# Raw weight loads issued by ScalarE behind earlier scalings, with a third raw place and five float32 places

## The chip, the cores and the metric

One core of a Trainium2 chip runs the kernel. The metric is the device time in microseconds, from launch to end. Engines are named as in the profile: PE (TensorE), DVE (VectorE), ACT (ScalarE), POOL (GpSimd), SP (SyncE).

## The reference

An attention with a threshold, and then two layers one after the other, each of two products with a function between them. The four weight matrices (`w_in` and `w_out` of each layer) come as float64, everything else as float32.

```python
def _attn_ref(q, k, v, tau):                 # 4 batches, 8 heads, 576 rows, 64 wide
    scores = scale * np.matmul(q, k.transpose(0, 1, 3, 2))
    thresh = np.max(scores, axis=-1, keepdims=True) - tau
    scores = np.where(scores >= thresh, scores, -1000000000.0)
    scores = scores - np.max(scores, axis=-1, keepdims=True)
    attn = np.exp(scores)
    attn = attn / (np.sum(attn, axis=-1, keepdims=True) + 1e-09)
    return np.matmul(attn, v).astype(np.float32)

def _moe_ref(x, w_in, w_out, a, b):          # 2304 tokens, 512 -> 2048 -> 512
    h = x @ w_in
    P = a[0] + a[1] * h + a[2] * h2 + a[3] * h3
    Q = 1.0 + np.abs(b[0]) * np.abs(h) + np.abs(b[1]) * h2
    return ((P / (Q + 1e-06)) @ w_out).astype(np.float32)

def _moe2_ref(x, w_in, w_out):
    h = x @ w_in
    g = np.where(pos, h, np.where(neg, 0.0, (h + beta) ** 2 / (4.0 * beta)))
    return (g @ w_out).astype(np.float32)

x = attention, heads side by side;  return _moe2_ref(_moe_ref(x))
```

## The kernel before

**Stages.** The tokens are worked on by batch (4), and each batch by three blocks of 192 tokens. For each batch the order is attention, first layer, second layer; the steps of a layer are 3 blocks x 8 chunks of the inner width. A step makes its first product (`first_product`, the matmuls of L843), the function (`rational` for the first layer, its first instruction is L724; `quadratic` for the second), and three steps later its second product (`second_product`, L857). The attention of the next batch runs beside the layers of the present one. The first batch's attention has a form of its own (`first_attention`), and beside it the weights are made.

**Weights.** Each of the two layers has 8 chunks, each chunk a half from `w_in` (x = 0) and one from `w_out` (x = 1): 32 halves, counted here from 0 to 31 in their order. Halves 0 to 15 belong to the first layer (`make_half`), 16 to 31 to the second (`stage_half`). A half is loaded raw (L241, 1024 KB, on SP), turned from float64 bits into float32 by three DVE instructions (`as_float`, L228 to L230), squared on PE (L253) for a bound on its size (L254, L187, L188), from which DVE makes a power of two (`root`, L168 to L172). ACT scales the float32 half in place (L217), and `split` makes two float16 parts of it, the high one on ACT (L208) and the low one by four subtractions on POOL (L212). The parts of the first layer stay in `wc` tiles and are also stored (L265); those of the second go into one of two `wh` tiles and are stored (L270), to be loaded when the second layer begins (L277).

**Buffers.** Raw halves lie in the tag "rw", two places; the raw `v` of the next batch (`prep_v`, L300 and L298) uses the same two. Float32 halves lie in "wt", three places (N_WT), the float16 halves of the second layer in "wh", two (N_WH). The q and k of a head pair lie raw in "rqk" and as float16 in "qk", one place each (`prep_pair`). All squares and bounds share one PSUM place, "aux".

**Order.** Instructions get a priority (`at`), and a planner that runs when the program is built lists them for each engine by readiness and priority. Buffers go round in the order of the source. Each engine and each queue then works its list in order: an instruction that waits holds up what is behind it. `tc.issue_after(ins)` puts what is issued in its block behind `ins` in the list of that engine, without a wait for its end.

Of the kernel before, what the change touches and what calls it, by code (L numbers as in the profile page):

```python
# [11 lines left out]
I32 = mybir.dt.int32  # L12
BF16 = mybir.dt.bfloat16
AF = mybir.ActivationFunctionType
# [21 lines left out]


ATTENTION = {1: (18, 50), 2: (60, 100), 3: (108, 147)}
WEIGHTS = (0, 20)
# [3 lines left out]
def tile_attention_moe_moe2(  # L43
# [20 lines left out]
    P = 128  # L64
# [140 lines left out]
    def split(hi, lo, src, scale=None, on_vector=True):  # L205
# [7 lines left out]
        elif on_vector:  # L213
            A.activation(hi, src, AF.Copy, scale=scale)
            V.scalar_tensor_tensor(lo, src, scale, hi, op0=ALU.mult, op1=ALU.subtract)
        else:
            A.activation(src, src, AF.Copy, scale=scale)  # L217
            split(hi, lo, src)

    def as_float(raw, name):  # L220

        if not wide:
            return raw
        src = raw.rearrange("p (n w) -> p n w", w=2)
        t = mp.tile([P, E], I32, name="wt" + name, tag="wt", bufs=N_WT)
        V.tensor_scalar(t, src[:, :, 1], 0x07FFFFFF, 3, op0=ALU.bitwise_and, op1=ALU.logical_shift_left)  # L228
        V.scalar_tensor_tensor(t, src[:, :, 1], -0x40000000, t, op0=ALU.bitwise_and, op1=ALU.bitwise_or)
        V.scalar_tensor_tensor(t, src[:, :, 0], 29, t, op0=ALU.logical_shift_right, op1=ALU.bitwise_or)  # L230
        return t.bitcast(F32)

    def convert(m, i, x, dst, on_vector):

        if x == 0:
            raw = rp.tile([P, KT, CF * words], raw_type, name=f"rw{m}_{i}_0", tag="rw")
            src = w_in_dram[m][:, i * CF * words : (i + 1) * CF * words].rearrange("(kt p) f -> p kt f", p=P)
        else:
            raw = rp.tile([P, NF, DM * words], raw_type, name=f"rw{m}_{i}_1", tag="rw")
            src = w_out_dram[m][i * CF : (i + 1) * CF, :].rearrange("(f p) d -> p f d", p=P)  # L240
        Q.dma_start(raw, src)  # L241
        name = f"{m}_{i}_{x}"
        src = as_float(raw.rearrange("p a b -> p (a b)"), name)
        hi, lo = dst[:, 0:E], dst[:, E : 2 * E]
# [10 lines left out]
        s = root("pw" + name, f_w[m][x][:, i : i + 1], everywhere("mw" + name, bound, 1), 2.0**64, even=m == 1 and x == 1)  # L255
        split(hi, lo, src, s, on_vector)
        if i == NCH - 1 and (m, x) != (0, 0):
# [700 lines left out]
```

## Time and profile before

| | us |
|---|---|
| median of 3 runs | 1245.84 |
| lowest, highest | 1241.46, 1250.6 |
| the profiled execution | 1242.5 |
| its span, first to last instruction | 1240.7 |
| busy PE, DVE, ACT, POOL | 1091.9, 977.1, 842.9, 543.0 |

The profile is of one execution. Busy time is a sum over the span; which engine sets the time differs from stage to stage. A row of the timeline gives start and length in us, the engine, the line of the kernel, and in brackets how long the engine was idle before it and what ended that. A half is found in the timeline by counting its line's instructions from the start.

### The profile page before, as it was taken

To read this page: it belongs to the slowest core of one execution; us is meant where nothing else is said; L and a number is where in the kernel's file an instruction comes from. 1 tells how busy PE (TensorE), PEld (TensorE's weight loads), DVE (VectorE), ACT (ScalarE), POOL (GpSimd) and SP (SyncE) were. 2 spreads that over 40 slices of the span, in tenths; PEclk is the share of its full clock that TensorE was granted. 3 is DMA by queue.
4 is the path that set the end of the run, shared out by engine and by line. 5 is a ranking of instruction groups with operands and counts; after the bars stand their busy time and mean duration, and the time that the engine had idled before them with its cause. 6 is when DMAs were issued, how large, how long until landed. Compare 5 with 4: busy or idle time off the path is not lost.

```text
span 1240.7 us, 31727 instructions
## 1 busy us (share of the span) xinstructions
PE 1091.9 (88%) x12618; PEld 984.5 (79%) x12618; DVE 977.1 (79%) x2353; ACT 842.9 (68%) x1533; POOL 543.0 (44%) x700
## 2 busy tenths in 40 slices
PE   2787788588799999999888998998899999999998
PEld 1444455488688888899788898998788989999997
DVE  7767887899997777799997776899996768896431
ACT  2477776779785677777875776887766767775332
POOL 3424545675673556421464555223563653222221
PEclk9797898799899999999999999999999999999999
DMA  7656676734447465923596539513993478007000
GB/s 209 230 169 217 218 258 205 240 116 120 108 136 234 68 125 116 249 73 92 144 238 131 110 69 245 140 49 68 243 192 69 86 167 221 14 1 259 16 14 27
DMA packets 220341, 176.40 MB, mean 142 GB/s; under 512 B 182048, under 2 KB 193312, under 8 KB 212000
## 3 DMA queue, kind: packets, MB, share of 16 engines
q1 hardware_dynamic: 220192, 174.36, 52.7%
q8 instruction: 99, 1.62, 0.5%
q14 instruction: 50, 0.41, 0.1%
HBM read 106.83 MB, written 21.50 MB: 103 GB/s over the span
## 4 chain that ended last, share of the span: by engine, by line
PE 35%; DVE 19%; DMA 9%; ACT 6%; POOL 6%; issue 6%; SPq 1%; DVEq 0%; ACTq 0%; POOLq 0%
PE ph L843 15%; PE acc L857 15%; DMA eT<-hl 7%; POOL hl L395 3%; DVE e L384 2%; PE pv L410 2%; DVE t L731 2%; DVE t L726 2%; DVE sc L422 2%; DVE t L737 1%; DMA qkT<-qk 1%; DVE t L728 1%; POOL gg L212 1%; DVE t L727 1%; ACT hl L392 1%
## 5 line engine op out<-in xcount | busy, mean ns | idle before, releaser
L857 PE MATMUL acc<-gg,wc 128*128 128x192 f16 x4608 | 427.6, 247 | 9.8 <-POOL gg L212 6.4
L843 PEld LDWEIGHTS <-wc 128*128 128x128 f16 x4608 | 389.8, 99 | 37.4 <-issue 20.8
L857 PEld LDWEIGHTS <-wc 128*128 128x128 f16 x4608 | 383.4, 98 | 13.3 <-issue 12.0
L212 POOL TENSOR_TENSOR gg<-t,gg 128x384 f16<-128x384 f32 x192 | 193.3, 1008 | 380.0 <-ACT gg L208 330.0
L843 PE MATMUL ph<-xT,wc 128*128 128x192 f16 x2304 | 220.2, 253 | 29.7 <-DVE t L728 21.2
L843 PE MATMUL ph<-yT,wc 128*128 128x192 f16 x2304 | 215.9, 247 | 1.0 <-DVE rk_f L160 0.6
L395 POOL TENSOR_TENSOR hl<-e,hl 128x256 f16<-128x256 f32 x216 | 154.3, 735 | 0.0
L208 ACT CAST gg<-t 128x384 f16<-128x384 f32 x192 | 97.0, 508 | 68.8 <-DVE t L790 34.7
L789 DVE SCALAR_TENSOR_TENSOR t<-t,c 128x384 f32<-128x384 f32 x96 | 64.0, 667 | 77.3 <-ACT t L788 77.0
L384 DVE SCALAR_TENSOR_TENSOR e<-sc,nt,e 128x576 f32<-128x576 f32 x108 | 96.2, 891 | 31.9 <-ACT e L383 31.3
L393 POOL TENSOR_TENSOR hl<-e,hl 128x64 f16<-128x64 f32 x108 | 43.3, 401 | 145.0 <-ACT hl L392 141.4
L788 ACT ACTIVATE t<-ph,c 128x384 f32<-128x384 f32 x96 | 64.0, 667 | 51.6 <-PE ph L843 51.2
L383 ACT ACTIVATE e<-sc,nt,con 128x576 f32<-128x576 f32 x108 | 93.4, 865 | 7.4 <-POOL hl L395 1.3
L410 PE MATMUL pv<-v,eT 128*128 128x65 f16 (+3 forms) x1680 | 70.1, 194 | 26.8 <-DMA eT<-hl 26.6
L422 DVE TENSOR_SCALAR_CACHE_REDUCE sc<-s 128x576 f32<-128x576 f32 x108 | 80.9, 749 | 13.5 <-PE s L377 12.7
L410 PEld LDWEIGHTS <-eT 128*128 128x128 f16 (+1 forms) x1680 | 62.2, 100 | 36.1 <-DMA eT<-hl 33.8
L724 ACT ACTIVATE t<-ph,sc 128x384 f32<-128x384 f32 x96 | 55.2, 575 | 51.5 <-PE ph L843 50.0
L392 ACT CAST hl<-e 128x576 f16<-128x576 f32 x108 | 72.0, 668 | 25.9 <-DVE e L384 25.3
L731 DVE SCALAR_TENSOR_TENSOR t<-t,ka,t 128x384 f32<-128x384 f32 x96 | 70.1, 730 | 11.1 <-ACT t L730 10.8
L729 ACT ACTIVATE t<-t,lc 128x384 f32<-128x384 f32 x96 | 67.9, 708 | 15.4 <-DVE t L726 15.0
L212 POOL TENSOR_TENSOR wc<-wt,wc 128x256 f16<-128x256 f32 x64 | 55.3, 897 | 46.1 <-ACT wc L208 46.1
L212 POOL TENSOR_TENSOR wh<-wt,wh 128x256 f16<-128x256 f32 x64 | 59.7, 961 | 33.0 <-ACT wh L208 28.9
(231 smaller groups left out, 1901.7 us busy)
## 6 DMA issues: line engine op xcount, KB each, us to landing
wc<-scratch SPq DMA_DIRECT2D x56, 1024.0 KB, 5.8
rw<-in_moe_w_in_dram SPq DMA_DIRECT2D x16, 1024.0 KB, 5.7
rw<-in_moe_w_out_dram SPq DMA_DIRECT2D x16, 1024.0 KB, 5.1
scratch<-wc SPq DMA_DIRECT2D x8, 1024.0 KB, 5.1
scratch<-wh SPq DMA_DIRECT2D x16, 512.0 KB, 3.6
rqk<-in_q_dram SPq DMA_DIRECT2D x16, 256.0 KB, 3.6
rqk<-in_k_dram SPq DMA_DIRECT2D x16, 256.0 KB, 3.0
kT<-qkT SPq DMA_DIRECT2D x28, 144.0 KB, 2.5
```

What stands on the lines that cost most here:

```text
L208: A.copy(hi, src)
L212: G.tensor_tensor(lo[:, p], src[:, p], hi[:, p], op=ALU.subtract)
L383: A.activation(e, s, AF.Exp, bias=nb, scale=con[:, 0:1])
L384: V.scalar_tensor_tensor(e, s, th, e, op0=ALU.is_ge, op1=ALU.mult)
L392: A.copy(hi, e)
L395: G.tensor_tensor(lo_w[:, p], e[:, whole][:, p], hi[:, whole][:, p], op=ALU.subtract)
L410: T.matmul(pv[rows, 0:w], eT[:, c, cols], vv[:, h * NT + x if x < NT else H * NT + h, at : at + w], start=(n == 0), stop=(n == len(blocks) ...
L422: V.tensor_scalar(s, banks[:, 0:S], 1.0, -LARGEST, op0=ALU.mult, op1=ALU.max, accum_out=mx)
L729: A.activation(r, u, AF.Ln, bias=lc[:, 1:2], scale=lc[:, 0:1])
L731: V.scalar_tensor_tensor(s, s, ka[:, 0:1], r, op0=ALU.add, op1=ALU.mult)
L843: last = T.matmul(ph[:, f, :], w[:, wx, kt, f * P : (f + 1) * P], rhs, start=(n == 0), stop=(n == 3 * KT - 1))
L857: T.matmul(dst, w[:, wx, f, d * P : (d + 1) * P], gg[:, gx, f, :], start=(i == 0 and f == 0 and n == 0 and d % 2 == 0), stop=(i == NCH - 1 ...
```

## The change

Raw loads leave SP for ACT: `load_raw` issues them with `A.dma_start`, inside `tc.issue_after(scaled[k - back])`, where `scaled` holds the scaling instruction (L217 of before) of each half. `back` is 3 for halves 9 to 28 and 2 for the others. Seven halves (`THIRD`: 8, 11, 14, 17, 20, 23 and 26) are loaded in two parts, into the places of "rqk" and "qk", the other halves into "rw" as before. `as_float` converts part by part. While the first layer's weights are made, float32 halves go round over five places, three of "wt" and two of "wh"; from half 16 on they use "wt" alone. What is computed stays the same.

```diff
--- before.py
+++ after.py
@@ -35,6 +35,7 @@
 N_TEMP, N_POLY, N_WT, N_WH, N_GG, N_ROW, N_SC = 5, 3, 3, 2, 4, 3, 2
 
 
+THIRD = {divmod(n, 2) for n in range(8, 28, 3)}
 ATTENTION = {1: (18, 50), 2: (60, 100), 3: (108, 147)}
 WEIGHTS = (0, 20)
 
@@ -214,33 +215,57 @@
             A.activation(hi, src, AF.Copy, scale=scale)
             V.scalar_tensor_tensor(lo, src, scale, hi, op0=ALU.mult, op1=ALU.subtract)
         else:
-            A.activation(src, src, AF.Copy, scale=scale)
+            done = A.activation(src, src, AF.Copy, scale=scale).ins
             split(hi, lo, src)
-
-    def as_float(raw, name):
+            return done
+
+    turn = [0]
+    scaled = []
+
+    def as_float(raws, name, first):
 
 
 
         if not wide:
-            return raw
-        src = raw.rearrange("p (n w) -> p n w", w=2)
-        t = mp.tile([P, E], I32, name="wt" + name, tag="wt", bufs=N_WT)
-        V.tensor_scalar(t, src[:, :, 1], 0x07FFFFFF, 3, op0=ALU.bitwise_and, op1=ALU.logical_shift_left)
-        V.scalar_tensor_tensor(t, src[:, :, 1], -0x40000000, t, op0=ALU.bitwise_and, op1=ALU.bitwise_or)
-        V.scalar_tensor_tensor(t, src[:, :, 0], 29, t, op0=ALU.logical_shift_right, op1=ALU.bitwise_or)
+            return raws[0].rearrange("p a b -> p (a b)")
+        n = turn[0] % (N_WT + N_WH)
+        turn[0] += 1
+        if first and n >= N_WT:
+            t = mp.tile([P, E], I32, name="wt" + name, tag="wh", bufs=N_WH)
+        else:
+            t = mp.tile([P, E], I32, name="wt" + name, tag="wt", bufs=N_WT)
+        at = 0
+        for raw in raws:
+            src = raw.rearrange("p a (n w) -> p (a n) w", w=2)
+            to = t[:, at : at + src.shape[1]]
+            at += src.shape[1]
+            V.tensor_scalar(to, src[:, :, 1], 0x07FFFFFF, 3, op0=ALU.bitwise_and, op1=ALU.logical_shift_left)
+            V.scalar_tensor_tensor(to, src[:, :, 1], -0x40000000, to, op0=ALU.bitwise_and, op1=ALU.bitwise_or)
+            V.scalar_tensor_tensor(to, src[:, :, 0], 29, to, op0=ALU.logical_shift_right, op1=ALU.bitwise_or)
         return t.bitcast(F32)
 
-    def convert(m, i, x, dst, on_vector):
-
+    def load_raw(m, i, x):
         if x == 0:
-            raw = rp.tile([P, KT, CF * words], raw_type, name=f"rw{m}_{i}_0", tag="rw")
             src = w_in_dram[m][:, i * CF * words : (i + 1) * CF * words].rearrange("(kt p) f -> p kt f", p=P)
         else:
-            raw = rp.tile([P, NF, DM * words], raw_type, name=f"rw{m}_{i}_1", tag="rw")
             src = w_out_dram[m][i * CF : (i + 1) * CF, :].rearrange("(f p) d -> p f d", p=P)
-        Q.dma_start(raw, src)
+        name, a = f"{m}_{i}_{x}", src.shape[1]
+        if wide and (m * NCH + i, x) in THIRD:
+            raws = [pool.tile([P, a // 2, src.shape[2]], raw_type, name=f"r{tag}{name}", tag=tag, bufs=1)
+                    for pool, tag in ((rp, "rqk"), (ap, "qk"))]
+        else:
+            raws = [rp.tile([P, a, src.shape[2]], raw_type, name=f"rw{name}", tag="rw")]
+        k = (m * NCH + i) * 2 + x
+        back = 3 if wide and 8 < k < 29 else 2
+        with tc.issue_after(scaled[k - back]) if k >= back else nullcontext():
+            for n, raw in enumerate(raws):
+                A.dma_start(raw, src[:, n * a // len(raws) : (n + 1) * a // len(raws)])
+        return raws
+
+    def convert(m, i, x, dst, on_vector):
+
         name = f"{m}_{i}_{x}"
-        src = as_float(raw.rearrange("p a b -> p (a b)"), name)
+        src = as_float(load_raw(m, i, x), name, m == 0)
         hi, lo = dst[:, 0:E], dst[:, E : 2 * E]
         columns = m == 0 and x == 0
         bound = gram[:, i : i + 1] if columns else small(1, "mb" + name)
@@ -253,7 +278,7 @@
                 T.matmul(pg[:, c * P : (c + 1) * P], top[:, k, c], top[:, k, c], start=(k == 0), stop=(k == n - 1))
         V.tensor_reduce(bound, pg[:, 0 : parts * P], axis=AX.X, op=ALU.max)
         s = root("pw" + name, f_w[m][x][:, i : i + 1], everywhere("mw" + name, bound, 1), 2.0**64, even=m == 1 and x == 1)
-        split(hi, lo, src, s, on_vector)
+        scaled.append(split(hi, lo, src, s, on_vector))
         if i == NCH - 1 and (m, x) != (0, 0):
             f_max[m][x] = small(1, f"f_max{m}{x}", True)
             V.tensor_reduce(f_max[m][x], f_w[m][x], axis=AX.X, op=ALU.max)
```

## Rows read from the trace of the kernel before

**Rows 1.** Busy time by stretch: stretch, its us, busy us and count, clock, DMA.
```profile
100.00:225.00 125.00, 101.53 (x631) 66.52 (x630) 101.53 (x216) 89.17 (x139) 64.21 (x74) 0.87 0.65 227
225.00:375.00 150.00, 117.97 (x1298) 110.81 (x1298) 143.79 (x319) 122.30 (x222) 99.96 (x101) 0.90 0.47 142
375.00:512.00 137.00, 127.54 (x1710) 117.23 (x1708) 100.53 (x274) 93.47 (x178) 71.25 (x110) 1.00 0.64 147
```

**Rows 2.** L724, first instruction of each step, in two layers: ns, first and last start.
```profile
L724 ACT ACTIVATE t<-ph,sc x24: 558/565/586, 238.7 to 369.4; 128x384 f32<-128x384 f32 x24
...
L724 ACT ACTIVATE t<-ph,sc x24: 559/581/582, 512.1 to 627.4; 128x384 f32<-128x384 f32 x24
```

**Rows 3.** What works on raw halves, 100 to 250 us; waits: us, times.
```profile
L228 DVE TENSOR_SCALAR wt<-rw x22: 677/688/1145, 99.6 to 244.0; 128x1024 int32<-128x1024 int32 x22
...
L230 DVE SCALAR_TENSOR_TENSOR wt<-rw,wt x22: 1209/1220/1686, 102.3 to 249.0; 128x1024 int32<-128x1024 int32 x22
...
  POOL wh L212: 4.7, 5
  POOL wc L212: 1.7, 4
...
DMA to landing us min/median/max: 4.7/5.4/7.9
```

**Rows 4.** Timeline of DVE: start, us, engine, line, operation, tiles, idle time before it.
```profile
68.80 0.70 DVE L228 TENSOR_SCALAR wt<-rw 128x1024 int32<-128x1024 int32 x1
...
99.55 1.14 DVE L228 TENSOR_SCALAR wt<-rw 128x1024 int32<-128x1024 int32 x1 [0.56 <-POOL wc L212]
...
121.28 0.68 DVE L228 TENSOR_SCALAR wt<-rw 128x1024 int32<-128x1024 int32 x1
...
128.33 0.69 DVE L228 TENSOR_SCALAR wt<-rw 128x1024 int32<-128x1024 int32 x1
...
134.00 0.69 DVE L228 TENSOR_SCALAR wt<-rw 128x1024 int32<-128x1024 int32 x1 [0.37 <-POOL wc L212]
...
268.72 1.02 DVE L228 TENSOR_SCALAR wt<-rw 128x1024 int32<-128x1024 int32 x1
269.67 0.14 DVE L168 TENSOR_SCALAR f_w<-mw 128x1 int32<-128x1 int32 x1
```

**Rows 5.** Timeline of POOL, the subtractions of halves 8, 10, 11, 12.
```profile
118.57 2.56 POOL L212 TENSOR_TENSOR wc<-wt,wc 128x256 f16<-128x256 f32 x4 [10.93 <-ACT wc L208]
...
130.52 3.45 POOL L212 TENSOR_TENSOR wc<-wt,wc 128x256 f16<-128x256 f32 x4 [3.01 <-ACT wc L208]
136.52 3.51 POOL L212 TENSOR_TENSOR wc<-wt,wc 128x256 f16<-128x256 f32 x4 [2.56 <-ACT wc L208]
141.90 5.33 POOL L212 TENSOR_TENSOR wc<-wt,wc 128x256 f16<-128x256 f32 x4 [1.87 <-ACT wc L208]
```

**Rows 6.** Timeline of ACT, the scalings of halves 5, 8, 11 and 12.
```profile
90.94 1.14 ACT L217 ACTIVATE wt<-wt,pw_s 128x1024 f32<-128x1024 f32 x1
...
116.28 1.14 ACT L217 ACTIVATE wt<-wt,pw_s 128x1024 f32<-128x1024 f32 x1
...
133.08 1.15 ACT L217 ACTIVATE wt<-wt,pw_s 128x1024 f32<-128x1024 f32 x1 [0.17 <-DVE pw_s L172]
...
139.60 1.15 ACT L217 ACTIVATE wt<-wt,pw_s 128x1024 f32<-128x1024 f32 x1 [0.80 <-DVE pw_s L172]
```

**Rows 7.** Timeline of SP: loads of halves 11 and 31, and of v's second part.
```profile
111.08 0.37 SPq L241 DMA_DIRECT2D rw<-in_moe_w_out_dram  x1
...
250.24 0.38 SPq L241 DMA_DIRECT2D rw<-in_moe_w_out_dram  x1
...
277.95 1.32 SPq L298 DMA_DIRECT2D rv<-in_v_dram  x2
```

**Rows 8.** Timeline of ACT: scaling of half 29, first split of v.
```profile
279.75 1.15 ACT L217 ACTIVATE wt<-wt,pw_s 128x1024 f32<-128x1024 f32 x1
...
299.29 2.56 ACT L214 ACTIVATE v<-rv,v_s 128x512 f16<-128x512 f32 x4
```

## What the change should do to the time

> **What bounds the kernel now.** I read the busy time by stretch first. It splits the run into stages with different limits. From 100 to 225 us, while the first batch's attention runs, no engine is full: PE 101.5, DVE 101.5 and ACT 89.2 us busy of 125. From 225 to 375 DVE is busy 143.8 of 150, and PE only 118.0. In the next stretch PE leads again with 127.5 of 137 [rows 1]. So the place where DVE work sets the time is the first batch's first expert layer, and what DVE has to do there beside it: the last weight halves and the start of the next attention.
>
> The second view says what those weights cost. The first instruction of the 24 steps of that layer runs from 238.7 to 369.4 us, 130.7 us. The same 24 steps for the second batch, with attention beside them but no weights, take 512.1 to 627.4, 115.3 us [rows 2]. The difference, 15.4 us, is about what the weights still cost once that layer has begun, and the most that finishing them earlier can bring.
>
> The third view gives the pace of the weights. From half 8 on, 22 halves start their first DVE instruction between 99.6 and 244.0 us, 144.4/21 = 6.9 us a half. In this stretch DVE never waited for a raw half to land; what ended its waits was POOL, 4.7 + 1.7 us in nine times [rows 3]. That is the float32 buffer: half k writes into the buffer of half k-3, whose last reader is POOL's subtraction. The times show it: POOL's subtractions for halves 8, 10, 11 and 12 end at 121.13, 133.97, 140.03 and 147.23 [rows 5], and halves 11 and 13 begin on DVE at 121.28 and 134.00 [rows 4]. Raw halves are there earlier: half 11 is issued at 111.08 [rows 7], lands by the median 5.4 us later [rows 3], 116.5, and is begun at 121.28 [rows 4].
>
> **The change part by part.** *Five float32 buffers for the first 16 halves.* This takes away the wait just described for them. Instead of the end of half k-3, half k needs the end of half k-5.
>
> *Third raw place and the new place of the load.* What bounds a half next is its load, because it now stands behind the scaling of half k-3 on ACT (k-2 up to half 8 and from 29). Worked out on the times of before: the scaling of halves 8, 11 and 12 starts at 116.28, 133.08 and 139.60 [rows 6]. An issue takes 0.37 us [rows 7] and a landing 5.4 [rows 3], together 5.8, so halves 11, 14 and 15 would be there at 122.1, 138.9 and 145.4. The float32 buffers that they took in fact came free at 121.13, 140.03 and 147.23 [rows 5]. The differences are +0.9, -1.1 and -1.8 us, -0.7 on a trip of three halves, or -0.2 us a half. One wait takes the place of the other at nearly the same time. Bounds: if every half went from DVE to its scaling as fast as half 12 did (128.33 to 139.60, 11.3 us), a trip were 11.3 + 5.8 = 17.1 us, 5.7 a half, 1.2 less than now; if all took half 8's 16.7 us (99.55 to 116.28), 22.5 us, 7.5 a half, 0.6 more. I take -0.4 a half for halves 9 to 15, seven halves: -3 us (bounds -8 to +4).
>
> *The start.* Halves 5 to 7 are turned into float32 early today, half 7 at 68.80 [rows 4], though half 5 isn't scaled before 90.94 [rows 6]. In the new order half 7 is loaded only behind half 5's scaling, lands at 96.7, and half 8 behind half 6's; half 8 also waits for the buffers of the fourth q/k pair. So DVE leaves 3.1 us of half 7's work (0.69 + 1.22 + 1.22: L228, L230 [rows 3], and L229, which has as many elements and operands as L230) undone in an idle stretch and does it at 97 us, where half 8 stood at 99.55. I take +3 us (0 to +6).
>
> *Halves 16 to 31* have three float32 buffers as before, since the other two hold their float16 results. The float32 wait stays and the load lands at about the same moment, so a half waits for the later of two: 0 to +0.6 a half (the upper bound above, 7.5 less 6.9), I take +0.2 on 13 halves, +3 us (0 to +8).
>
> These three add to a shift of the last weights of +3 us (-8 to +18). It is paid where DVE is full. Seven us is one half more or less in that layer, and a half costs there between 2.2 us (15.4 us for the seven halves, 25 to 31, that at 6.9 us a half up to 268.7 [rows 4] fall into the stretch from 225) and 3.1 us, its large DVE instructions. So +3 us of shift is +1 us of time.
>
> *The tail.* From half 29 two raw places remain. Half 31's load stands at 250.24 today [rows 7] and comes behind half 29's scaling, 279.75 [rows 8]; landed at 285.6. The second part of the next batch's v takes that raw place, 277.95 today [rows 7], 9.2 us after DVE began half 31 at 268.72 [rows 4]: then 295, 17 us later. The split of v on ACT, 299.29 [rows 8], follows from it. What hides this is that DVE is full anyway, with steps of the layer to do in place of it, and that the second layer, which needs the weights, begins when the first one's last steps do, near 369.4 [rows 2]. I take +1 us (0 to +17).
>
> *Added instructions.* Seven halves in two parts are 21 more DVE instructions; between nothing and 0.14 us each, what the one-column instruction on half 29's f_w takes [rows 4], up to 3 us: +1, mostly in the stage where DVE isn't full. 39 issues on ACT at 0.37 us are 14 us of its sequencer; each stands behind a scaling of 1.15 us [rows 6], beside which it can run: 0 (to +4, were it all to lie in the open and carry as ACT's share of 122.3 in 150 [rows 1] suggests for the quarter after 225). Behind an issue on ACT stand the scaling and casts of the next halves and the exponentials of the attention; as the raw place was read out before half k-3 could be scaled, the issue itself doesn't wait. On SP, 32 issues and their waits go. Nothing behind them was late: stores go out when POOL is done, and the rest of SP's work in this stretch is sparse. 0.
>
> **A rule against it.** Today half 11's load is issued 10.2 us before use (111.08 to 121.28 [rows 7, 4]); in the new order it would be issued at 116.3, with no slack left. The Trainium skill, "DMA: Bandwidth & Descriptors", Rules for kernel authors, says to issue a transfer early, compute, and wait for it late, so that its fixed cost overlaps. By the row the load arrives just as the half is due and costs nothing. By the rule it loses that cover. That is the third rival below.
>
> **Sum.** 1 + 1 + 1 = +3 us on the profiled execution's 1242.5 (span 1240.7): 1245.5. The median of the three runs lies 3.3 above that execution, in a spread of 9 us between them; I go half of the way and give 1247 as the median to be expected.
>
> **The rivals.**
> 1. *The weights get ahead.* The five buffers and the third place take the pace to the lower bound, 5.7 us a half, in the stage where DVE has 23 us of 125 idle. Then half 16 comes 8 us earlier, and since the order is planned as a whole, the later halves and the attention close up too; all 15.4 us can come back. For it: DVE and POOL are both far from full before 225. Against it: halves 16 to 31 keep the float32 wait. Time: 1247 - 3 - 15 = 1229; half of it is 1237.
> 2. *The tail decides.* v comes 17 us later and the next attention, which goes on until about 512 us beside the second layer, ends so much later. For it: in that stretch PE is at 127.5 of 137 [rows 1], so there is little to fill a hole with. It decides once the split of v comes later than the first attention rows need it, some 20 us after 299.29. Time: 1244 + 17 = 1261.
> 3. *Loads just in time.* Where the landing is slower than the planned order expects (up to 7.9 us against 5.4 [rows 3]), DVE stands still in order, with the attention's reductions behind it: 1 to 2.5 us for a half on 23 halves, 23 to 57 us of pace, three to eight halves more in the full layer at 2.2 to 3.1 us: +7 to +25, middle 15. Time: 1245 + 15 = 1260. Against it: three halves are in flight, and the worked times give -0.7 us on a trip.
>
> **How the numbers follow.** Forecast (within about 8 us of 1247) 0.48, rival 1 0.28, rival 2 0.12, rival 3 0.12. A measurement of this kernel can tell about 1%, 12.5 us, from no change: below 1233.4 is faster, above 1258.3 slower. Of rival 1 some 0.21 lies below, and 0.03 of the forecast, since a new order of the whole program moves later stages by some us either way. Of rivals 2 and 3 0.19 lies above, and 0.03 of the forecast. So faster 0.24, slower 0.22, same 0.54. The range reaches to both sides: 1228 to 1264 leaves a tenth out on each. The forecast's own range is 1239 to 1255.
>
> **What would show it.** The loop: first DVE instructions of halves 9 to 15 at 6.5 us a half, no longer waiting for POOL but for raw landings; at under 6 rival 1 holds. Half 7's first DVE instruction near 97 us instead of 69. The tail: half 31's load behind 275 us, the second part of v's load near 295; an end of the second layer's first batch later than 512 speaks for rival 2. DVE waits for raw landings of over 20 us in all speak for rival 3. The 24 steps of the first layer at 125 to 135 us speak for the forecast, near 115 for rival 1. The prediction is wrong at its root if the scaling comes much sooner after the DVE work than 11 to 17 us.

## The result and the profile after

The changed kernel takes 1260.16 us (median of 8 runs, 1250.93 to 1264.74), the kernel before 1248.98 (8 runs). The ratio is 1.0095, 95% interval 1.0066 to 1.0123: about 1% slower, and 1 lies outside the interval. The profiled execution of after took 1259.39 us, span 1257.3, which is 16.6 more than the span of before. That is more than the 11.2 between the medians, since the profiled execution of before (1242.5) was one of its faster ones. Here and below, stretches of time are read from one execution per kernel, while executions of one kernel lie up to 14 us apart (1250.93 to 1264.74). Differences of a few us between stretches therefore have no interval.

The first table cuts the span at two points that every kernel here has: the first step of the first batch's first layer, and the first step of the same layer for the second batch. All three columns are us of the profiled execution.

| | up to the first layer | both layers of batch 1 | from there to the end |
|---|---|---|---|
| before [rows 2] | 238.7 | 273.4 | 728.6 |
| after | 249.0 (+10.3) | 281.1 (+7.7) | 727.2 (-1.4) |

The points for after are these, from the first instruction of the 24 steps (ns, then first and last start), the same view as [rows 2]. The 24 steps take 130.2 us (130.7 before), and the second batch's take 115.1 (115.3 before): in both batches the first layer keeps its length and begins later. The 7.7 us of the middle column lie behind its last step: from there to the second batch's first step it was 142.7 us (369.4 to 512.1), now 150.9 (379.2 to 530.1).

```profile
L749 ACT ACTIVATE t<-ph,sc x24: 557/564/581, 249.0 to 379.2; 128x384 f32<-128x384 f32 x24
...
L749 ACT ACTIVATE t<-ph,sc x24: 560/579/582, 530.1 to 645.2; 128x384 f32<-128x384 f32 x24
```

Busy time by stretch, which answers to [rows 1]. From 100 to 225 us all engines do less: PE 95.4 (101.5 before), DVE 95.6 (101.5), ACT 82.9 (89.2). Work is lost here, although no engine is full.

```profile
100.00:225.00 125.00, 95.35 (x593) 61.31 (x593) 95.55 (x216) 82.86 (x126) 58.60 (x67) 0.86 0.65 218
225.00:375.00 150.00, 115.32 (x1184) 104.37 (x1182) 142.86 (x301) 118.56 (x207) 96.60 (x97) 0.90 0.47 144
375.00:512.00 137.00, 125.33 (x1654) 114.54 (x1652) 108.32 (x285) 96.44 (x188) 77.55 (x110) 0.99 0.71 152
```

Where in it? Each head pair of the first attention ends with a division, whose logarithm is one instruction on ACT. Its four starts in before are 45.3, 44.8 and 45.2 us apart; in after 56.6, 41.8 and 48.2. The pair that ends at 147.28 has lost 11.3 us, the third gains 3.0 and the fourth loses 3.0. First the timeline of ACT in before:

```profile
91.99 0.76 ACT L605 ACTIVATE rd<-d,least 128x576 f32<-128x576 f32 x1
137.31 0.78 ACT L605 ACTIVATE rd<-d,least 128x576 f32<-128x576 f32 x1
182.14 0.78 ACT L605 ACTIVATE rd<-d,least 128x576 f32<-128x576 f32 x1
227.30 0.77 ACT L605 ACTIVATE rd<-d,least 128x576 f32<-128x576 f32 x1
```

Then the timeline of ACT in after, with the stretch in which the pair loses its time:

```profile
90.67 0.78 ACT L630 ACTIVATE rd<-d,least 128x576 f32<-128x576 f32 x1
...
103.01 0.37 ACTq L262 DMA_DIRECT2D rrqk<-in_moe_w_in_dram  x1
...
109.70 0.74 ACT L609 ACTIVATE et<-st,con 128x576 f32<-128x576 f32 x1
115.94 0.39 ACTq L262 DMA_DIRECT2D rqk<-in_moe_w_in_dram  x1
116.37 0.74 ACT L609 ACTIVATE et<-st,con 128x576 f32<-128x576 f32 x1 [5.93 <-DMA kT<-qk]
...
126.53 0.74 ACT L606 ACTIVATE low<-st,con 128x576 bf16<-128x576 f32 x1 [8.79 <-PE st L603]
...
147.28 0.77 ACT L630 ACTIVATE rd<-d,least 128x576 f32<-128x576 f32 x1
189.05 0.78 ACT L630 ACTIVATE rd<-d,least 128x576 f32<-128x576 f32 x1
237.26 0.78 ACT L630 ACTIVATE rd<-d,least 128x576 f32<-128x576 f32 x1
```

Half 8 is the first with two parts. Its first part is issued at 103.01, its second not before 115.94. The exponential behind it (L609) has an idle time of 5.93 us put down to `kT<-qk`: not that the exponential needs this transpose, but that the issue ahead of it on ACT's queue needs the place "qk", which the transposes of the last q/k pair still read. The trace books such a wait on the next instruction that counts as busy.

The timeline of DVE over the same place and at half 31, to set beside [rows 4]:

```profile
106.07 0.70 DVE L242 TENSOR_SCALAR wt<-rw 128x1024 int32<-128x1024 int32 x1 [1.30 <-DMA rw<-in_moe_w_out_dram]
...
119.79 0.43 DVE L242 TENSOR_SCALAR wt<-rrqk 128x512 int32<-128x512 int32 x1 [9.53 <-DMA rrqk<-in_moe_w_in_dram]
...
120.74 0.68 DVE L549 TENSOR_REDUCE mx<-sm 128x1 f32<-128x512 f32 x1
...
318.69 1.16 DVE L242 TENSOR_SCALAR wt<-rw 128x1024 int32<-128x1024 int32 x1
```

Half 7 begins at 106.07 (68.80 before) and half 8 at 119.79 (99.55). For 9.53 us DVE stands for the first part of half 8, and behind it in DVE's list stands the attention's reduction (L549). The chain of work that ended last runs through exactly this landing; it is the longest piece of the chain in that stretch, and a second landing follows 10 us later (start, us, what):

```profile
103.01 16.69 DMA rrqk<-in_moe_w_in_dram
...
129.24 5.56 DMA rw<-in_moe_w_in_dram
```

Why 16.69 us for 512 KB? From 100.10 to 106.24 us the loads of halves 7 and 9, the first part of half 8 and a store of finished weights are issued, and the DMA share of the view by stretch is 1.07 from 102 to 114 us (0.65 over the 125 us around it). That this crowd stretches the load is a reading, which a4 tests below. The transposes of the last q/k pair are in the same crowd: from issue to landing the transposes take 2.8 to 14.0 us, where before they took 2.9 each time. First the view by stretch of after, then its transposes of q and k (count, ns of an issue, first and last start, and the time to landing), and last the landing of the transposes in before:

```profile
102.00:114.00 12.00, 9.49 (x60) 6.02 (x60) 5.80 (x9) 6.97 (x10) 7.10 (x8) 1.00 1.07 310
```

```profile
L375 SPq DMA_TRANSPOSE qT<-qk x2: 1296/1303/1310, 82.5 to 100.5; - x2
L375 SPq DMA_TRANSPOSE kT<-qk x2: 1316/2766/4217, 83.9 to 101.9; - x2
...
DMA to landing us min/median/max: 2.8/4.8/14.0
...
DMA to landing us min/median/max: 2.9/2.9/2.9
```

The lateness is older than half 8. Halves 2 to 7, too, are now loaded behind the scaling two halves back: half 3 begins on DVE at 49.55 after a wait for its landing, against 35.12, and ACT scales the last raw q/k pair of the first attention at 97.2, against 87.2. The last transpose of q is issued 8.6 us later (100.46, before 91.89). First before, then after, the first DVE instruction of half 3 and the scalings of raw q and k:

```profile
35.12 0.69 DVE L228 TENSOR_SCALAR wt<-rw 128x1024 int32<-128x1024 int32 x1
L217 ACT ACTIVATE rqk<-rqk,qkr_s x8: 759/768/776, 13.9 to 87.2; 128x576 f32<-128x576 f32 x8
...
49.55 1.10 DVE L242 TENSOR_SCALAR wt<-rw 128x1024 int32<-128x1024 int32 x1 [4.34 <-DMA rw<-in_moe_w_out_dram]
L218 ACT ACTIVATE rqk<-rqk,qkr_s x8: 757/761/774, 17.7 to 97.2; 128x576 f32<-128x576 f32 x8
```

This part does belong to the place of the load. In the seven kernels here that load weights on ACT, the last of these scalings starts between 97.0 and 98.3 us; in the seven that load them all on SP, between 87.2 and 90.0.

Taken over the first 250 us, these are waits of after (engine, instruction, what it waited for; us in all, times, longest). DVE's waits for raw landings come to 9.8 + 9.5 + 7.1 + 1.3 = 27.7 us there, 29.3 with those after 250; before they were 6.1 in all, and none of them after 100 us [rows 3]. The wait for POOL, 4.1, is a little less than the 4.7 + 1.7 of [rows 3]. Below the waits of after stand DVE's two of before for raw landings.

```profile
ACT low L606 <- PE st L603: 19.8, 11, 8.8
...
DVE wt L242 <- DMA rw<-in_moe_w_in_dram: 9.8, 3, 4.5
DVE wt L242 <- DMA rrqk<-in_moe_w_in_dram: 9.5, 1, 9.5
...
DVE wt L242 <- DMA rw<-in_moe_w_out_dram: 7.1, 4, 4.3
...
ACT et L609 <- DMA kT<-qk: 5.9, 1, 5.9
...
DVE wt L242 <- POOL wh L213: 4.1, 4, 1.8
...
DVE wt L242 <- DMA rrqk<-in_moe_w_out_dram: 1.3, 1, 1.3
...
DVE wt L228 <- DMA rw<-in_moe_w_out_dram: 4.5, 2, 3.5
...
DVE wt L228 <- DMA rw<-in_moe_w_in_dram: 1.6, 2, 1.3
```

The last place is SP's queue (to set beside [rows 7]): the next batch's first raw q is loaded at 249.87, against 94.8 before, since halves with two parts hold both places of q and k until DVE has converted half 26, which it begins at 245.3. The second part of v comes at 323.59 (277.95), the first transpose of the next attention's exponentials at 362.32 (319.4), 43 us later. Two rows of before stand first.

```profile
94.79 0.43 SPq L321 DMA_DIRECT2D rqk<-in_q_dram  x1
...
319.37 1.31 SPq L397 DMA_TRANSPOSE eT<-hl  x1
...
249.87 0.39 SPq L346 DMA_DIRECT2D rqk<-in_q_dram  x1
...
323.59 1.32 SPq L323 DMA_DIRECT2D rv<-in_v_dram  x2
...
362.32 1.31 SPq L422 DMA_TRANSPOSE eT<-hl  x1
```

### The profile page after: what moved, and what is told of

The parts are those of the page before. It is cut to its first block, busy times and chain, and to the rows that moved or that the text cites. A ratio compares the mean times of both kernels' runs of the same rounds, so it can differ in the third digit from the quotient of the medians.

```text
span 1257.3 us, 31734 instructions
## 1 busy us (share of the span) xinstructions
PE 1093.0 (87%) x12618; PEld 981.6 (78%) x12618; DVE 982.5 (78%) x2374; ACT 842.7 (67%) x1533; POOL 545.2 (43%) x700
## 4 chain that ended last, share of the span: by engine, by line
PE 39%; DVE 29%; DMA 15%; ACT 7%; issue 5%; POOL 4%; SPq 1%; ACTq 0%; DVEq 0%; POOLq 0%
PE ph L868 15%; PE acc L882 15%; DMA eT<-hl 6%; DMA qkT<-qk 2%; DVE t L756 2%; DVE e L409 2%; DVE sc L447 2%; DMA rw<-in_moe_w_out_dram 2%; DVE t L751 2%; PE pv L435 2%; POOL hl L420 2%; DVE t L753 2%; DVE t L762 2%; DVE t L752 1%; PE pv L618 1%
## 5 line engine op out<-in xcount | busy, mean ns | idle before, releaser
L882 PEld LDWEIGHTS <-wc 128*128 128x128 f16 x4608 | 380.8, 98 | 14.1 <-issue 13.2
L213 POOL TENSOR_TENSOR gg<-t,gg 128x384 f16<-128x384 f32 x192 | 196.7, 1026 | 374.3 <-ACT gg L209 317.1
L868 PE MATMUL ph<-xT,wc 128*128 128x192 f16 x2304 | 216.2, 251 | 16.4 <-DVE t L753 13.1
L749 ACT ACTIVATE t<-ph,sc 128x384 f32<-128x384 f32 x96 | 55.1, 574 | 45.2 <-PE ph L868 44.9
L754 ACT ACTIVATE t<-t,lc 128x384 f32<-128x384 f32 x96 | 67.7, 707 | 17.5 <-DVE t L751 17.0
L756 DVE SCALAR_TENSOR_TENSOR t<-t,ka,t 128x384 f32<-128x384 f32 x96 | 70.9, 738 | 10.1 <-ACT t L755 9.8
L751 DVE SCALAR_TENSOR_TENSOR t<-t,qc 128x384 f32<-128x384 f32 x96 | 69.0, 719 | 4.1 <-ACT t L749 3.9
```

The costliest lines, as they stand in the source:

```text
L213: G.tensor_tensor(lo[:, p], src[:, p], hi[:, p], op=ALU.subtract)
L751: V.scalar_tensor_tensor(u, u, qc[:, 0:1], u, op0=ALU.add, op1=ALU.mult)
L756: V.scalar_tensor_tensor(s, s, ka[:, 0:1], r, op0=ALU.add, op1=ALU.mult)
L868: last = T.matmul(ph[:, f, :], w[:, wx, kt, f * P : (f + 1) * P], rhs, start=(n == 0), stop=(n == 3 * KT - 1))
L882: T.matmul(dst, w[:, wx, f, d * P : (d + 1) * P], gg[:, gx, f, :], start=(i == 0 and f == 0 and n == 0 and d % 2 == 0), stop=(i == NCH - 1 ...
```

## The experiments

All runs are set against the kernel before on the same chip, whose median was 1247 to 1249. A gives the us of the profiled execution up to the first layer, B both layers of the first batch, C the rest, each as a difference from before (238.7, 273.4, 728.6). "Landings" is DVE's idle time ended by raw landings, over the whole run; the last two columns are the second part of v's load and the scaling of half 31, in us from the start.

| kernel | us | ratio [95%] | A | B | C | landings | v | half 31 |
|---|---|---|---|---|---|---|---|---|
| before | | 1 | 0 | 0 | 0 | 6.1 | 278 | 295 |
| after | 1260.16 | 1.0095 [1.0066, 1.0123] | +10.3 | +7.7 | -1.4 | 29.3 | 324 | 341 |
| a1_half8_in_rw | 1279.12 | 1.0249 [1.0216, 1.0281] | +10.1 | +19.8 | +8.6 | 30 | 321 | 347 |
| a2_tail_on_sync | 1266.93 | 1.0159 [1.0127, 1.0191] | +5.2 | +13.8 | +0.6 | 22 | 298 | 341 |
| a3_both | 1269.81 | 1.0189 [1.0151, 1.0226] | +8.6 | +15.2 | +4.9 | 27 | 311 | 341 |
| a4_half9_later | 1270.08 | one run | +18.0 | +11.6 | -2.0 | 25 | 318 | 352 |
| b5_loads_on_sync | 1260.34 | 1.0092 [1.0064, 1.0121] | +11.7 | +2.8 | +3.9 | 9.1 | 263 | 289 |
| b1_five_floats_only | 1260.42 | 1.0096 [1.0061, 1.0132] | +16.0 | -5.0 | +4.4 | 13.2 | 258 | 272 |
| b3_place_of_load_only | 1286.67 | 1.0284 [1.0231, 1.0337] | -1.7 | +31.9 | +17.5 | 31.4 | 362 | 377 |
| d1_late_first_pair | 1254.33 | 1.0060 [1.0028, 1.0092] | -1.0 | +8.9 | +0.9 | 6.6 | 279 | 302 |
| n1_nudge_first_halves | 1262.12 | 1.0134 [1.0090, 1.0178] | +4.9 | +3.4 | +10.6 | 1.3 | 273 | 312 |
| n2_nudge_second_halves | 1256.46 | 1.0080 [1.0047, 1.0112] | +3.3 | +5.9 | +4.4 | 7.0 | 272 | 331 |
| c3_half8_by_sync | 1264.92 | 1.0139 [1.0084, 1.0195] | +6.4 | +10.7 | +3.3 | 27 | 307 | 322 |
| e1_floats_low_priority | 1255.34 | 1.0063 [1.0034, 1.0091] | +9.3 | -5.3 | +6.2 | 14 | 249 | 262 |

**Theory S, two spots.** The trace of after shows two places that look like the whole loss: half 8 behind the q/k places at 100 to 120 us, and the tail, where the loads of halves 29 to 31 and with them v come 40 us later. If S held, each mended spot would bring some us back. The rival J says that the loss is spread over all halves, since each is loaded just in time.

a1 begins the third place with half 11:

```diff
-THIRD = {divmod(n, 2) for n in range(8, 28, 3)}
+THIRD = {divmod(n, 2) for n in range(11, 28, 3)}
...
-        back = 3 if wide and 8 < k < 29 else 2
+        back = 3 if wide and 10 < k < 29 else 2
```

> The changed kernel, but the third raw place is first used by half 11 instead of half 8; half 8 goes into rw and halves 8 to 10 are loaded behind the scaling two back. Theory S (the loss sits at two spots: about 11 us where half 8 takes the q/k places, between 100 and 120 us, and about 5 us at the tail): the second head pair of the first attention takes 45 to 48 us again (from one divide's first logarithm to the next; 56.6 in the changed kernel, 45.3 before), the first layer begins near 240 us, the time falls by 8 to 11 us to about 1250. Rival J (loads just in time: the loss is spread over all halves as waits for landings): the first layer still begins at 246 or later, the time stays within 4 us of 1260.

It is 1.5% above after, not below. The wait for `kT<-qk` is gone and the pair that lost 11.3 us has 50.1 in place of 56.6, yet A is as late as in after, and B grows by 12 us more.

a2 lets SP load halves 29 to 31, behind nothing; a3 joins both edits.

```diff
-        with tc.issue_after(scaled[k - back]) if k >= back else nullcontext():
+        by_sync = k > 28
+        with tc.issue_after(scaled[k - back]) if k >= back and not by_sync else nullcontext():
...
-                A.dma_start(raw, src[:, n * a // len(raws) : (n + 1) * a // len(raws)])
+                (Q if by_sync else A).dma_start(raw, src[:, n * a // len(raws) : (n + 1) * a // len(raws)])
```

> The changed kernel, but halves 29 to 31 are loaded by SP as before, behind nothing. Theory S: v's second part is issued near 285 to 295 us instead of 323.6, the first transpose of the second batch's rows near 325 to 335 instead of 362, and the first step of the second batch's first layer near 525 instead of 530: the time falls by 4 to 6 us to about 1255. Rival N (the late v is made good anyway, since DVE is full there): v and the first transpose come earlier as said, but the time stays within 2 us of 1260.

> Both edits at once: third place from half 11, halves 29 to 31 on SP. Theory S: the two add up, about 1245, ratio to the kernel before 0.995 to 1.000. Rival J: 1255 or more, ratio above 1.005.

In a2 v's second part comes 25 us earlier than in after, and the first transpose of the next attention's exponentials doesn't move: 362.8 (362.3). The time is 0.6% above after. a3 is above it too. So in a2 the lateness of v is not what holds the next attention, and at neither spot does the time do what S expects.

a4 keeps the third place at half 8 and loads half 9 behind the scaling of half 7 (`9 < k < 29`), to thin out the crowd at 103 to 110 us. It tells apart whether ACT stands for the place or for the crowd.

> The changed kernel with one number changed: half 9 is loaded behind the scaling of half 7 instead of half 6, so that not three loads start within 3 us beside the last q/k transposes. Half 8 still takes the q/k places. Theory B (too many transfers at once: 2.5 MB of loads, a store and the transposes between 100 and 116 us): the transposes of the last pair land in under 7 us instead of 14, ACT waits under 3 us for the place instead of 5.9, DVE under 3 us for half 8's first part instead of 9.5; second pair 46 to 49 us. Rival P (the place itself: ACT stands before half 8's second part until the transposes are through, whatever else runs): ACT's wait stays at 5 us or more and the second pair above 52 us.

DVE's wait for the first part of half 8 falls from 9.5 to 3.5 us, the transposes still take up to 11.8 us to land, and ACT's wait for them stays, 6.3 us. So, as far as one execution shows, DVE's wait came with the load of half 9 in the crowd, ACT's from the place; the slow transposes don't need that load. The time of its one run doesn't fall.

**Theory J, parts alone.** Now the parts of the change one by one. b5 is after with every raw load back on SP, without `issue_after`; the two kinds of places stay. b1 leaves out the third raw place as well (`THIRD = set()`), so only five float32 places are left of the change. b3 is the other side: two raw and three float32 places as before, and the load on ACT behind the scaling of two halves back.

```diff
-        with tc.issue_after(scaled[k - back]) if k >= back else nullcontext():
+        with nullcontext():
...
-                A.dma_start(raw, src[:, n * a // len(raws) : (n + 1) * a // len(raws)])
+                Q.dma_start(raw, src[:, n * a // len(raws) : (n + 1) * a // len(raws)])
```

That is b5. b1 is b5 with `THIRD = set()`. b3 is after with `THIRD = set()` and these lines:

```diff
-        if first and n >= N_WT:
+        if False:
...
-        back = 3 if wide and 8 < k < 29 else 2
+        back = 2
```

> The changed kernel with one part undone: all raw loads are issued by SP again, behind nothing, as soon as their place is free; third place and five float32 places stay. Theory J (just in time: loads behind a scaling land when the half is already due, and DVE stands still in order): DVE waits for raw landings 10 us or less in all (29.3 in the changed kernel, 6.1 before), the first attention's last divide comes near 227 to 231 us (237.3; 227.3), the time falls to 1246 to 1252. Rival H (the held q/k places cost the time, not the place of the load): waits may fall, but the first transpose of the second batch stays at 355 or later and the time at 1257 or more.

> The kernel before with five float32 places for halves 0 to 15 alone: loads on SP, two raw places. Theory J: nothing of the loss is here; raw halves become the bound of the first 16 halves at 5 to 6 us a half, half 16 is scaled near 160 instead of 169, the time is 1240 to 1249. Rival F (more float32 places make the planned order crowd the first attention): the last divide comes at 232 or later and the time is 1255 or more.

> The kernel before with only the place of the load changed: ACT issues every raw load behind the scaling of the half two back; two raw places, three float32 places. Theory J: a half's cycle gets the landing in the open (two halves in some 22 us instead of three in 21), DVE waits for raw landings more than 30 us, half 16 is scaled at 195 or later instead of 169, the last halves come behind 350 us and the time is 1265 or more. Rival: if the landing is hidden by other work, half 16 is scaled before 180 and the time is below 1255.

b3 is the largest effect of the study, +2.84%. What it does can be read from its first DVE instruction of each half (ns, first and last start; then what ended the idle time before it): 16 of 32 halves find DVE standing for a landing, and half 31 begins at 353.7 in place of 268.72 [rows 4].

```profile
L242 DVE TENSOR_SCALAR wt<-rw x32: 676/1008/1202, 8.4 to 353.7; 128x1024 int32<-128x1024 int32 x32
...
  DMA rw<-in_moe_w_in_dram: 21.8, 10
  DMA rw<-in_moe_w_out_dram: 9.6, 6
```

So the place of the load by itself costs what rival 3 of the prediction gave it, and more: half 31 is scaled 83 us later. In after, with the added places and the load of most halves three back, about two thirds of the time come back (half 31 scaled at 341 rather than 377, ratio 1.0095). This is where the Trainium skill's rule ("DMA: Bandwidth & Descriptors", Rules for kernel authors: issue a transfer early, compute, wait for it late) agrees with the trace: 6.1 us of waits for landings turn into 31.4.

b3 also shows two things that bear on after. Its second head pair takes 55.4 us, nearly the 56.6 of after, though no half lies in the q/k places there. And 29.0 us of the waits for landings come before the first layer, which still begins at 237.0, before the 238.7 of the kernel before. By then DVE has begun 22 halves rather than 29; what is left is paid behind the layer's last step, 170.1 us to the second batch's first step rather than 142.7. These are the layer's 24 steps and DVE's idle time up to 237 us:

```profile
L749 ACT ACTIVATE t<-ph,sc x24: 557/572/589, 237.0 to 372.2; 128x384 f32<-128x384 f32 x24
...
  DMA rw<-in_moe_w_in_dram: 19.4, 7
  DMA rw<-in_moe_w_out_dram: 9.6, 6
```

So waits for landings alone don't make the first layer late; how the order shares the stretch between weights and attention counts too.

But b5 keeps J from being shown as the cause of after's 1%. With the loads on SP the waits for raw landings come to 9.1 us rather than 29.3, in the waits of its first 250 us:

```profile
DVE wt L242 <- POOL wh L213: 7.6, 8, 2.9
...
DVE wt L242 <- DMA rw<-in_moe_w_out_dram: 6.0, 3, 4.3
...
DVE wt L242 <- DMA rrqk<-in_moe_w_in_dram: 1.8, 1, 1.8
DVE wt L242 <- DMA rw<-in_moe_w_in_dram: 1.3, 1, 1.3
```

Half 31 is scaled 52 us earlier than in after and the next attention's first exponentials go out at 306 rather than 362, and the time is the same: 1260.34 against 1260.16. With the added places there, it makes no difference that can be measured whether ACT or SP loads.

b1 says the same of the third place: five float32 places alone cost +0.96%. Here the weights do get ahead, by 22 us at half 31:

```profile
L218 ACT ACTIVATE wt<-wt,pw_s x32: 1132/1145/1154, 16.5 to 272.3; 128x1024 f32<-128x1024 f32 x32
```

And the first layer's 24 steps take 129.5 us still (254.7 to 384.2; 130.7 in [rows 2]). What is late is its beginning, by 16.0 us, because the first attention's last division comes at 238.6 rather than 227.3. ACT's `low` waits for PE 30.5 us there (21.2 before). One reading is that weights that are ready sooner take their turn on DVE and ACT ahead of the attention: DVE has begun all 32 halves when the layer begins, where it had begun 29 in the kernel before.

e1 asks whether that is so: b1, with the priority of halves 8 to 15 lowered.

```diff
-            with at(2.4 * (2 * NCH - len(halves)) - 40):
+            with at(2.4 * (2 * NCH - len(halves)) - (28 if len(halves) <= NCH else 40)):
```

> Five float32 places alone (loads on SP, two raw places), with halves 8 to 15 planned 12 steps later in priority, so that the attention goes first wherever both are ready. Theory F (with more float32 places the halves crowd the first attention: its pairs took 49.5, 46.5 and 45.5 us, its first layer began at 254.7): the pairs take 44 to 46 us, the first layer begins at 238 to 243, the time falls from 1260.4 to 1250 or less. Rival R: the pairs stay at 46 us or more on average and the time at 1255 or more.

Its time is 1255.34, ratio 1.0063 against 1.0096 of b1, with intervals that overlap, and 6.7 of A come back (248.0 rather than 254.7). But the weights don't get later, rather earlier (half 31 scaled at 261.6), so the edit didn't make what it was meant to try. The time fits the rival (1255 or more), the pairs, 45.8 us on average, don't quite (46 or more): nothing is settled.

**Theory H, the late first pair.** In after the second batch's first q/k pair is loaded at 249.87 rather than 94.8. d1 does only this, in the kernel before: that pair's loads stand behind the load of half 30.

```diff
+        loads.append(Q.dma_start(raw, src).ins)
...
+        with tc.issue_after(loads[30]) if b == 1 else nullcontext():
-        ahead = [prep_pair(b, 0)]
+            ahead = [prep_pair(b, 0)]
```

> The kernel before with one thing made late: SP issues the loads of the second batch's first q/k pair behind the load of half 30 (243.8 us) instead of at 94.8, as the third raw place does in the changed kernel by holding the q/k places (loads at 249.9). Theory H: the pair's transpose moves from 289.6 to 320 or later, the first transpose of the second batch's rows from 319 to 345 or later, and the time rises by 4 to 8 us to 1252 to 1256. Rival J: the pair has time enough either way; the first transpose stays before 330 and the time within 3 us of 1248.

The time goes up by 0.6%, as H expected, but not by its way: the first exponentials' transpose stays where it was (319.0, before 319.4), and what is longer is B.

**Controls.** Each edit makes the planner write a new order of all engines. How much is that alone? n1 and n2 change nothing but a priority by 0.4: no wait, place, queue or instruction is added (n1 is the first pair of lines, n2 the second).

```diff
-            with at(2.4 * (2 * NCH - len(halves)) - 40):
+            with at(2.4 * (2 * NCH - len(halves)) - 39.6):
...
-WEIGHTS = (0, 20)
+WEIGHTS = (0.4, 20.4)
```

> A control: the kernel before with the priority of the first layer's halves moved by 0.4 of a step (40 becomes 39.6) and nothing else; no wait, place or queue is changed, only the planned order. Theory R (the planned order of before is a good one among near ones, and most orders cost about 1%, so that part of the changed kernel's loss is that its order is another): the time rises by 5 to 15 us, the head pairs of the first attention are no longer all near 45 us. Rival M (the loss is made by the places and the new place of the load alone): the time stays within 4 us of 1249 and the pairs at 45 us.

> A second control: the kernel before with the priority of the second layer's halves moved by 0.4 of a step (0 to 20 becomes 0.4 to 20.4). Theory R: the time differs from 1249 by 4 us or more, upward more likely. Rival M: within 4 us.

They cost +1.34% and +0.80%, with intervals that overlap that of after. A new order alone is worth as much as the whole change. The +0.6% of d1 is therefore not shown to come from the late pair, and the same holds against S: a2 lies 12 us above what S expects, which a new order could explain. Only a1 and a3, 29 and 25 us above, lie farther off than either control moved the time.

**One spot, mended by itself.** c3 lets SP load half 8 alone (the edit of a2 with `by_sync = k == 8`). Theory S once more, at its plainest spot; the rival R is that this pair is mended, others get longer, and the time stays.

> The changed kernel, but half 8's two parts are loaded by SP, behind nothing, so that ACT doesn't stand before the q/k place; all other loads stay on ACT. Theory P (ACT's wait for the place, 5.9 us, with the 8.8 and 9.5 us of ACT and DVE behind it): the second head pair takes 45 to 49 us instead of 56.6, the first layer begins at 239 to 243 instead of 249.0, the time falls by 6 to 10 us to 1250 to 1254. Rival R: that pair is mended, but others get longer, and the time stays at 1257 or more.

ACT's wait for `kT<-qk` is gone, DVE's for the first part of half 8 falls to at most 2.6 us, the pair takes 52.2 us in place of 56.6 (45 to 49 were expected) and the first layer begins 3.9 us earlier than in after. The time is 1264.92, not lower, as R expects: in the one execution, B is 3.0 us longer than in after and C 4.7. With the controls beside it, the lost gain has no cause that is shown.

## Why the prediction was right and where it was wrong

The forecast was no change within 1%, 1247 us, range 1228 to 1264. The median ratio is +0.95%, its interval reaches from +0.66% to +1.23%, and 1260.16 lies in the range but outside the forecast's own range of 1239 to 1255. The sum of +3 us on the profiled execution met +16.6, and 11.2 between the medians. That the change stayed within 1% is in part luck: a rise clear of noise came where none was forecast, the range held it because it was wide enough for the rivals at either end, and the shift of the weights, on which the sum was built, was far off while the price that it was given didn't show. The prediction's own bound for slower, 1258.3, was passed; it was set from three runs with a median of 1245.84, and the eight that count now have 1248.98. By its steps:

- **The pace of halves 9 to 15 (-3 us): wrong in sign.** From half 8's first DVE instruction to half 16's it is 59.5 us in after (119.79 to 179.28) and 57.0 before (99.55 to 156.52): 7.4 a half where 6.5 was expected. A wait for landings did take the place of part of the one for POOL (4.1 us are left of 6.4), but it won nothing; behind half 8 it is 5.2 us in three waits up to 250 us.
- **"The issue itself doesn't wait" (0): wrong.** It holds for the places "rw", which the sentence looked at. The third place is that of q and k, and its readers are the transposes. One issue held ACT for 5.93 us. The length of an issue, 0.37, was right: 374 ns at the least, 380 in the median for the 1024 KB loads.
- **The start (+3, bound +6): the term that was mis-sized.** Half 7 begins at 106.07 (97 expected), half 8 at 119.79, 20.2 us later than before. The step saw halves 5 to 7 only. But halves 2 to 4 are tied to earlier scalings too, so that half 3 begins 14.4 us late and half 5 is scaled at 100.25 (90.94). And it took the median landing of [rows 3], 5.4 us, where the first load into the q/k places took 16.69.
- **Halves 16 to 31 (+3): no sign of it up to half 28.** From half 16's first DVE instruction to half 28's it is 80.9 us (179.28 to 260.16), before 81.5 (156.52 to 237.97).
- **The shift of the last weights (+3, bound +18) and its price (+1): the first far too small, the second not seen.** Half 28 begins 22 us later, 12 if counted from the layer's own beginning, and half 31 50 us (318.69). At 2.2 to 3.1 us for each 7 us, 22 us were to cost 7 to 10 us in the first layer; its 24 steps take 130.2 us, 0.5 less. (Of the seven halves put into that stretch, DVE begins only five after 225 us in before.) What grew is the stretch behind the layer, by 8.2 us.
- **Idle time taken for slack: no term for the 10.3 us of A.** The three terms were turned into a shift of the weights and paid only in the stage where DVE is full. But before 225 us DVE and ACT serve the weights and the attention by one list each, and a wait for weights also holds the attention's work behind it, as at half 8, although neither engine is full. Rival 3 named this mechanism ("with the attention's reductions behind it") but priced it in the full layer as well. That these waits make the 10.3 us is not shown: b3 has 29.0 us of them and begins the layer 1.7 us early, b5 has 9.1 and b1 13.2, and they begin it 11.7 and 16.0 late.
- **15.4 us as "the most that finishing them earlier can bring": not borne out.** In b1 and e1 the weights end 22 and 33 us earlier and the layer's 24 steps take 129.5 and 137.1 us. Both layers together gain only about 5 us (B -5.0 and -5.3), and A loses more. Rival 1 had its first half come true there (the weights get ahead), and not its second. In the control n1 the same 24 steps take only 118.2 us, with half 31 scaled 18 us later than before and the next attention's first exponentials going out at 355.8. So the 15.4 us are not simply what the weights cost; in n1 they come back by another order, and are lost behind the layer.

```profile
L724 ACT ACTIVATE t<-ph,sc x24: 555/570/589, 243.6 to 361.8; 128x384 f32<-128x384 f32 x24
```

- **The tail (+1, bound 17 us later): mis-sized, the lateness and the price.** Half 31 is loaded at 311.2 (behind 275 was expected), v's second part at 323.6 (295): 45.6 us later, not 17. That the q/k places are held until half 26 is converted was not seen at all. The next attention's first exponentials go out 43 us late, and behind the first layer 8.2 us are lost where +1 was expected, so the cover named in the prediction held for most of the 43 us, not for all. Rival 2's sign came (the second batch's first layer begins at 530.1, behind 512), but 10.3 of these 18.0 us are A's, and v is not what holds the next attention: in a2 v comes 25 us earlier and the first transpose doesn't move.
- **Added instructions (+1): borne out.** A first instruction of half the size takes 427 ns in the median, 694 for the whole: 0.16 us more for two than for one, expected were 0 to 0.14. The 24 steps of the layer, 125 to 135 expected, take 130.2.
- **A new order "moves later stages by some us either way": too small.** The two controls moved the time by 10 and 17 us (0.80% and 1.34%), both to the slower side.

Of the rivals, the third had its sign: over 20 us of waits for landings were named, 29.3 came, and its time was 1260. That a load tied to a late scaling makes DVE stand, and costs time, is shown for the place of the load alone (b3), though not by way of the full layer, whose 24 steps take 135.2 us there. It is not shown as the cause of after's 1%: b5 takes those waits away and is as slow.

**What stays open.** That the loss of after sits in A (+10.3) and B (+7.7), in B behind the first layer's last step, which waits stand in A, and that the tie makes the first attention's q and k 10 us late by 97 us, is shown. Which of these waits cost time is not, and how much of the 11 us each part of the change is worth isn't either: the added places without ACT's loads, the five float32 places without the third raw one, and a mere change of a priority all come to +0.8 to +1.3%. No run beat the kernel before, so its order is a good one among near ones, and part of the 1% may be nothing but having left it. Telling that apart would take one fixed order for all variants, which wasn't tried; nor was a third raw place with memory of its own.

## What to carry to other kernels

Before an idle share is called slack, look at which chains pass through the engine in that stage: a wait put into a list that two chains share holds whatever of the other chain stands behind it, and which of the two ends late is then a matter of the order. When loads are tied to later events, follow the tie from the first load on, not only where the new buffers begin. A transfer tied to a late event needs more places to stay hidden: here the tie alone cost 2.8%, tie and places together 1%, and the places without the tie the same 1%. When a planner writes the whole order, run one or two edits that change only the order before a change of 1% is given a cause.

## What the runs showed of the hardware

A DMA transpose that landed after 2.9 us each time in the kernel before took up to 14.0 us from issue to landing, and a load of 512 KB 16.69 us, when both were under way with 1024 KB transfers at a DMA share of 1.07 (102 to 114 us of after). In b3, where no load goes into the q/k places, a transpose took 10.9 us beside such loads. The issue of a 1024 KB load on ACT takes about as long as on SP (380 ns in the median, and 370), and while an issue waits for its place the activations behind it wait too: 5.93 us here, which the trace books on the next activation.
